# Quarter products in place of full ones in the first layer of seven experts, with the work between the engines set out anew

## The chip, the cores and the metric

The kernel runs on one core of a Trainium2 chip. The metric is the device time of one execution in microseconds (us). The kernel before takes 992.46 us, the median of three runs (991.57 to 992.61).

## The reference, cut to what matters

Local attention gives 4608 tokens of 512 numbers each. A gate then picks two of eight experts for each token, and an expert is two matrix products with a relu between them:

```python
    for e in range(E):
        for k in range(2):
            mask = top2[:, k] == e
            if not mask.any():
                continue
            h = np.maximum(x[mask] @ w1[e], 0.0)
            out[mask] += top2_w[mask, k, None] * (h @ w2[e])
```

All of it is float32: `x` is 4608 x 512, `w1[e]` is 512 x 1024, `w2[e]` is 1024 x 512. About 1152 tokens go to each expert.

## The kernel before, in words

**Stages.** Attention, gate and routing come first and overlap with expert 0. From the middle of expert 0 on TensorE does little but expert products. An expert has a fixed number of places for tokens (`CAPS`, L30): 1216 for the first two, 1184 for three, 1152 for three. More tokens than that go through an extra loop at the end (L844), which runs zero times here; its count `n_over` is worked out in L829 to L843, after the last expert.

**Numbers in two parts.** A float32 operand is split into a high part (a ScalarE copy to `fp32r`) and a low part (a VectorE subtraction, operand minus high part). `three` (L298) multiplies two such operands with three matmuls: high by high, high by low, low by high. Each matmul loads a 128 x 128 piece as weights and streams the other operand past it.

**Blocks.** `blocks_tail` (L51) cuts the list of experts 1 to 7 into three blocks of 384 tokens; what is over 1152 (64 or 32 tokens, the tail) joins the first block. `BL` (L149) is the list of all blocks. Expert 0 has blocks of its own (`blocks_of`, L37), the last one with a tail of 64.

**First layer** (`layer1`, L307): for each of 8 pieces of 128 hidden units, 4 pieces of the 512 inputs, 3 matmuls each, so 96 matmuls in a block, each streaming the block's 384, 416 or 448 tokens. ScalarE applies relu and writes the high part `hh` (L323), VectorE the low part `hl` (L324). A tail's hidden units go to `hf` instead (L321).

**Second layer** (`layer2`, L346): per tile of 128 tokens 24 matmuls of 512 columns. `weigh` (L340) scales the result on VectorE (L343), and `store` (L270) adds it to the output with an indirect DMA that POOL issues (L272). A tail goes through `tail2` (L327) with small matmuls (L334) before the block's tiles.

**What surrounds them.** POOL gathers the tokens ahead of time, four indirect DMAs to a tile (`gather_some`, L248, L260), at most `LEAD` = 7 tiles ahead, in 5 + 3 buffers. `x_tile` (L279) turns a tile on VectorE (L292) and splits it (L295 ScalarE, L296 VectorE). Weights arrive by DMAs that SP issues (`w_load`, L120) into four staging buffers `st`, and are split by `w_split` (L130: L137 ScalarE, L138 VectorE). The order on every engine is the order of the program. The main loop (L751) hands small pieces of this work to hooks that run between groups of matmuls: the tiles of the next block during the first layer or, in the middle block, during the second; the split of `w2` during the first layer of the middle block; the split of the next expert's `w1` in the second layer.

Of the kernel before, what the change touches and what calls it, by code (L numbers as in the profile page):

```python
# [60 lines left out]
def kernel(ctx, tc, qT, kT, vh, wgn, noise, w1, w2, out, caps=CAPS):  # L61
# [4 lines left out]

    xbuf = dram.tile([NROWS, DM], FT, name="xbuf")
# [3 lines left out]
    jp = consts.tile([P, P], FT, name="jp")  # L71
# [3 lines left out]
    before = consts.tile([P, P], BF, name="before")  # L75
    nc.vector.tensor_scalar(before, jp, 0.0, None, op0=OP.is_gt)
    ones = consts.tile([P, P], BF, name="ones")
# [4 lines left out]
    row = consts.tile([P, P], FT, name="row")  # L82
    nc.gpsimd.iota(row, pattern=[[1, P]], base=0, channel_multiplier=0, allow_small_or_imprecise_dtypes=True)
    e_row = row[:, 0:NE]

    row_p = consts.tile([P, P], FT, name="row_p")
    nc.gpsimd.iota(row_p, pattern=[[NE, P]], base=0, channel_multiplier=0, allow_small_or_imprecise_dtypes=True)
    row_je = consts.tile([P, NLIST, NE], FT, name="row_je")
# [52 lines left out]
    pg = ExitStack()  # L141
    gate = pg.enter_context(tc.tile_pool(name="gate", bufs=1, side="right"))
# [5 lines left out]
    assert all(len(b) == nb for b in blocks)  # L148
    BL = [(e, b) for e in range(NE) for b in range(nb)]  # L149
    NBL = len(BL)  # L150
    NJ = NLIST
    BN = max(sum(r for _, r in b) for bs in blocks for b in bs)
    LEAD = 7
# [10 lines left out]
    later_xg = []  # L164
    xg = ctx.enter_context(tc.tile_pool(name="xg", bufs=5))
    bx0 = ctx.enter_context(tc.tile_pool(name="bx0", bufs=1))
# [3 lines left out]
    acc = consts.tile([P, 2, NL], FT, name="acc")  # L170
# [18 lines left out]
    WIDE = {"tr": (0, 1), "l1": (0, 2, 3, 4), "l2": (1, 5, 6, 7)}  # L189

    def bank(what, among=None):
        among = among or (BANKS if rot["l2"] < 6 else WIDE)[what]
# [86 lines left out]
    def x_tile(i, k, at=None):  # L279
# [5 lines left out]
        if i < NPE:  # L285
            src = (bank("tr") if at is None else PS[:, at, :]).rearrange("p (d n) -> p d n", d=ND)[:, :, 0:r]
            for d in range(ND):
                nc.tensor.transpose(src[:, d, :], x[0:r, d * P:(d + 1) * P], ident[0:r, 0:r])  # L288
            oh, ol = xh[:, :, s], xl[:, :, s]
        else:  # L290
            y = xy.tile([P, DM], FT, name="y")
            nc.vector.transpose(y[:, 0:4 * r], x[:, 0:4 * r])  # L292
            src = y[:, 0:4 * r].rearrange("p (t b c) -> p b t c", b=ND, c=32)
            oh, ol = (a[:, :, s].rearrange("p b (t c) -> p b t c", c=32) for a in (xh, xl))
# [3 lines left out]
    def three(p, w, w_s, x, x_s, first, last, flip=False):  # L298

        (wh, wl), (xh, xl) = w, x  # L300
        for n, (a, b) in enumerate(((wh, xh), (wh, xl), (wl, xh)) if not flip else ((wh, xh), (wl, xh), (wh, xl))):
# [3 lines left out]
            nc.tensor.matmul(p, a, b, start=first and n == 0, stop=last and n == 2)  # L305

    def layer1(i, hook, hook_d=lambda f, d: None):  # L307
# [3 lines left out]
        for f in range(NF):  # L311
# [645 lines left out]
```

## Time and profile before

| | |
|---|---|
| median of 3 runs | 992.46 us |
| the profiled execution: its own time | 993.31 us |
| its span, first to last instruction | 991.5 us |
| TensorE matmul busy (PE) | 953.3 us, 96% |
| weight loads (PEld) | 854.4 us, 86% |
| VectorE (DVE) | 458.3 us, 46% |
| ScalarE (ACT) | 307.8 us, 31% |
| GpSimd (POOL) | 485.2 us, 49% |
| granted TensorE clock, mean | 0.991 |

PE is matmul and PEld weight load, both on TensorE. The busy time of an engine is the time in which at least one of its instructions is on record as running. Matmuls are pipelined: the record of one lasts until its end, while the next has already begun, so the pace of TensorE is read from starts and not from durations. `L305` is line 305 of the kernel; since every expert matmul is recorded in `three`, they all have this one line and are told apart by their tiles and widths. A span of 1.00 in the column PEclk is the full 2.4 GHz.

### The profile page before, as it was taken

Reading aid. Unit: us, or ns where it says so; the run is one execution under the profiler, and the core shown is the slowest. Engines: PE = TensorE matmul, PEld = TensorE weight load, DVE = VectorE, ACT = ScalarE, POOL = GpSimd, SP = SyncE. Lnnn points to the kernel's source line nnn. Section 1 sums busy time; section 2 is a strip of 40 time slices with the busy share of each in tenths; the row PEclk is TensorE's granted clock in tenths of the full one; section 3 lists DMA queues with packets and bytes.
Section 4 is the critical chain, followed back from the end, with each engine's and each line's share of the span. In section 5 each row is a group of like instructions: output and inputs, shape, how many; then the busy total and the mean of one; then the engine's idle time right before and its main releaser. Section 6 shows DMA issues by size and latency. Waiting matters only on the chain.

```text
span 991.5 us, 18556 instructions
## 1 busy us (share of the span) xinstructions
PE 953.3 (96%) x7353; PEld 854.4 (86%) x7353; DVE 458.3 (46%) x1001; ACT 307.8 (31%) x689; POOL 485.2 (49%) x619
## 2 busy tenths in 40 slices
PE   6788989999999999999999999999999999999995
PEld 5666779998798998998899899989998999899984
DVE  6678876643444442534253435343444344434311
ACT  4667865312232321322132213122312231223100
POOL 1033635426677876177517772676167616601111
PEclk9999999999999999999999999999999999999998
DMA  9998968332513462245214522552245224511213
GB/s 330 376 308 299 317 224 326 63 114 57 144 47 85 108 152 49 47 120 149 51 35 128 149 49 37 134 141 58 70 94 141 58 71 94 136 20 22 32 23 43
DMA packets 60362, 121.54 MB, mean 123 GB/s; under 512 B 9280, under 2 KB 10176, under 8 KB 60272
## 3 DMA queue, kind: packets, MB, share of 16 engines
q1 hardware_dynamic: 40112, 81.64, 23.3%
q0 software_dynamic: 20160, 38.69, 21.0%
q8 instruction: 58, 0.95, 0.4%
q14 instruction: 32, 0.26, 0.1%
HBM read 81.56 MB, written 38.73 MB: 121 GB/s over the span
## 4 chain that ended last, share of the span: by engine, by line
PE 84%; DVE 1%; issue 0%
PE PS L305 82%; PE PS L334 1%; PE PS L590 1%; PE PS L288 0%; DVE gmi L518 0%; PE PS L222 0%; PE PS L464 0%; PE PS L476 0%; DVE o L343 0%; DVE xs L449 0%; PE PS L224 0%; DVE gm L514 0%; PE PS L457 0%; DVE nf L836 0%; PE PS L537 0%
## 5 line engine op out<-in xcount | busy, mean ns | idle before, releaser
L260 POOL DMA_INDIRECT xg<-xbuf,piece x257 | 265.9, 1035 | 71.4 <-issue 65.0
L305 PE MATMUL PS<-xh,w1h 128*128 128x384 f32 (+2 forms) x768 | 263.1, 343 | 0.0
L305 PE MATMUL PS<-xh,w1l 128*128 128x384 f32 (+2 forms) x768 | 260.8, 340 | 0.0
L305 PE MATMUL PS<-xl,w1h 128*128 128x384 f32 (+2 forms) x768 | 260.7, 339 | 0.0
L272 POOL DMA_INDIRECT out<-o,lid x73 | 116.1, 1591 | 244.2 <-DVE o L343 232.7
L305 PE MATMUL PS<-w2h,hh 128*128 128x512 f32 x584 | 228.6, 391 | 0.0
L305 PE MATMUL PS<-w2h,hl 128*128 128x512 f32 x584 | 227.7, 390 | 0.0
L305 PE MATMUL PS<-w2l,hh 128*128 128x512 f32 x584 | 227.5, 390 | 0.0
L323 ACT ACTIVATE hh<-PS 128x384 fp32r<-128x384 f32 (+1 forms) x192 | 93.9, 490 | 362.3 <-PE PS L305 361.5
L324 DVE SCALAR_TENSOR_TENSOR hl<-PS,hh 128x384 fp32r<-128x384 f32 (+1 forms) x192 | 106.9, 558 | 180.8 <-ACT hh L323 180.8
L343 DVE TENSOR_SCALAR o<-PS,lwt 128x512 f32<-128x512 f32 x73 | 54.7, 749 | 233.5 <-PE PS L305 233.5
L305 PEld LDWEIGHTS PS<-xh,w1h 128*128 128x128 f32 x768 | 144.7, 188 | 2.7 <-issue 0.8
L305 PEld LDWEIGHTS PS<-xl,w1h 128*128 128x128 f32 x768 | 144.7, 188 | 1.8
L305 PEld LDWEIGHTS PS<-xh,w1l 128*128 128x128 f32 x768 | 144.5, 188 | 1.0
L305 PEld LDWEIGHTS PS<-w2h,hl 128*128 128x128 f32 x584 | 109.2, 187 | 23.6
L305 PEld LDWEIGHTS PS<-w2h,hh 128*128 128x128 f32 x584 | 109.2, 187 | 23.1 <-issue 0.8
L305 PEld LDWEIGHTS PS<-w2l,hh 128*128 128x128 f32 x584 | 109.2, 187 | 22.4
L295 ACT ACTIVATE xh<-y 128x512 fp32r<-128x512 f32 x67 | 41.2, 615 | 105.1 <-DVE y L292 105.1
L296 DVE TENSOR_TENSOR xl<-y,xh 128x512 fp32r<-128x512 f32 x67 | 44.9, 671 | 48.0 <-ACT xh L295 48.0
L598 POOL TENSOR_SCALAR gohp<-row_p,gpf 128x128 f32<-128x128 f32 x36 | 24.8, 721 | 85.0 <-DVE gpf L582 76.7
L292 DVE STREAM_TRANSPOSE y<-xg 128x512 f32<-128x512 f32 x67 | 45.6, 680 | 3.5 <-DMA xg<-xbuf,piece 3.5
L138 DVE TENSOR_TENSOR w2l<-st,w2h 128x512 fp32r<-128x512 f32 x64 | 44.3, 693 | 0.0
(139 smaller groups left out, 780.6 us busy)
## 6 DMA issues: line engine op xcount, KB each, us to landing
st<-in_w SPq DMA_DIRECT2D x56, 512.0 KB, 3.4
out<-zero SPq DMA_DIRECT2D x37, 256.0 KB, 3.3
vb<-in_vh SPq DMA_DIRECT2D x36, 260.0 KB, 4.7
qp<-in_qT SPq DMA_DIRECT2D x36, 256.0 KB, 5.6
kb<-in_kT SPq DMA_DIRECT2D x36, 256.0 KB, 5.7
xbuf<-xs SPq DMA_DIRECT2D x36, 256.0 KB, 4.3
xg<-xbuf,piece POOLq DMA_INDIRECT x257, 2.8
st<-in_w SPq DMA_DIRECT2D x16, 256.0 KB, 4.2
```

The lines of the kernel that those rows point to most:

```text
L138: (eng or nc.vector).tensor_sub(lo[:, s], st[:, s], hi[:, s].bitcast(FT))
L260: nc.gpsimd.indirect_dma_start(out=XG[e, j][:, t * P:(t + 1) * P], out_offset=None, in_=xpieces, in_offset=bass.IndirectOffsetOnAxis(ap=pi ...
L272: s = nc.gpsimd.indirect_dma_start(out=to, out_offset=bass.IndirectOffsetOnAxis(ap=rows, axis=0), in_=o, in_offset=None, compute_op=OP.add)
L292: nc.vector.transpose(y[:, 0:4 * r], x[:, 0:4 * r])
L295: nc.scalar.activation(oh, src, AF.Copy)
L296: nc.vector.tensor_sub(ol, src, oh.bitcast(FT))
L305: nc.tensor.matmul(p, a, b, start=first and n == 0, stop=last and n == 2)
L323: nc.scalar.activation(hh[:, 0:m], p, AF.Relu)
L324: nc.vector.scalar_tensor_tensor(hl[:, 0:m], p, 0.0, hh[:, 0:m].bitcast(FT), op0=OP.max, op1=OP.subtract)
L334: nc.tensor.matmul(p[32 * q:32 * q + 32, 0:P], HF[0][:, f, 32 * t:32 * t + 32], w[:, q * P:(q + 1) * P], start=(f == 0), stop=(f == NF - 1))
L343: nc.vector.tensor_scalar(o[0:r], p[0:r], weights_of(i, j)[0:r], None, op0=OP.mult)
L598: nc.gpsimd.tensor_scalar(ohp[:, 0], row_p, pf[:, 0, 0, r:r + 1], None, op0=OP.is_equal)
```

## The change

Experts 1 to 7 compute their first layer by seven products of quarter matrices in place of eight. The 512 x 1024 matrix `w1` is cut in four (inputs by hidden units), a block of tokens in four (inputs by tokens), and sums of quarters are multiplied: Strassen's scheme in the form with fifteen additions. Four of the additions are on quarters of `w1` and four on quarters of the tokens, the others are on results.

- An expert has two blocks in place of three: 512 tokens and the tail, and 640 tokens. Each half of the tokens is 256 (288 or 272 with the tail's half), or 320 wide. `layer1s` runs, for each of seven products `m`, four pieces `f` of 128 hidden units, two pieces `d` of the inputs, three matmuls.
- Products accumulate in two chains of PSUM banks, `a` in banks 0 to 3 and `b` in banks 4 to 7 (`CHAIN`). Between two products of chain `a` ScalarE copies a bank to a buffer `u`; VectorE adds chain `b` to `u`, and relu and low part are made from the sum. A tail's part of a sum goes through POOL.
- `weights_work` and `rows_work` list the additions and splits as small tasks, and the loop over blocks hands them out at given steps of both layers (`SPLITS`, `TASKS`, and the spacings 1.6 and 0.7). The whole of the next block's rows but three splits is made in a second layer; the three (`rows_later`) at steps 5, 9 and 20 of the first layer that uses them.
- `weigh` scales on ScalarE from the last block of expert 0 on. `tail2` comes after the first tile. `LEAD` is 5 in place of 7 and all gathered tiles use the 5 buffers.
- The count of overflowing rows is computed on VectorE after the routing and not after the last expert; the load of the count and the branch stay where they were.
- Buffers of the gate and of the constants move to a pool that is closed after the routing. Expert 0's own first layer is as before.

```diff
...
-    full = [(j, P) for j in range(cap // P)]
-    out = [full[n:n + 3] for n in range(0, len(full), 3)]
-    if cap % P:
-        out[0] = out[0] + [(cap // P, cap % P)]
-    return out
+    assert cap // P == 9
+    tail = [(9, cap % P)] if cap % P else []
+    return [[(j, P) for j in range(4)] + tail, [(j, P) for j in range(4, 9)]]
...
-            W[e, which, c] = (wpool.tile([P, 1024], FR, name=f"w{which}h{c}"),
-                              wpool.tile([P, 1024], FR, name=f"w{which}l{c}"))
+            h, l = (f"a{c}", f"a{4 + c}") if which == 1 else (f"w2h{c}", f"w2l{c}")
+            W[e, which, c] = wpool.tile([P, 1024], FR, name=h), wpool.tile([P, 1024], FR, name=l)
...
-    BN = max(sum(r for _, r in b) for bs in blocks for b in bs)
-    LEAD = 7
+    BN = max(sum(r for _, r in b) for b in blocks[0])
+    LEAD = 5
...
-        n = rot["xg"] = rot["xg"] + (i >= NPE)
-        XG[e, blocks[e][b][k][0]] = (later_xg[0] if n % 8 in (1, 2, 3) and i >= NPE else xg).tile([P, DM], FT, name="xg")
+        XG[e, blocks[e][b][k][0]] = xg.tile([P, DM], FT, name="xg")
...
-            r = blocks[e][b][-1][1] % P if e else 0
-            m = n - r
-            if r:
-                nc.scalar.activation(HF[0][:, f, 0:r], p[:, m:n], AF.Relu)
-                p = p[:, 0:m]
-            nc.scalar.activation(hh[:, 0:m], p, AF.Relu)
-            nc.vector.scalar_tensor_tensor(hl[:, 0:m], p, 0.0, hh[:, 0:m].bitcast(FT), op0=OP.max, op1=OP.subtract)
+            nc.scalar.activation(hh[:, 0:n], p, AF.Relu)
+            nc.vector.scalar_tensor_tensor(hl[:, 0:n], p, 0.0, hh[:, 0:n].bitcast(FT), op0=OP.max, op1=OP.subtract)
...
-        nc.vector.tensor_scalar(o[0:r], p[0:r], weights_of(i, j)[0:r], None, op0=OP.mult)
+        if i >= NPE - 1:
+            nc.scalar.activation(o[0:r], p[0:r], AF.Copy, scale=weights_of(i, j)[0:r])
+        else:
+            nc.vector.tensor_scalar(o[0:r], p[0:r], weights_of(i, j)[0:r], None, op0=OP.mult)
         store(e, out, rows_of(i, j)[0:r], o[0:r])
 
-    def layer2(i, hook):
+    def layer2(i, hook, hh, what=None):
         e, b = BL[i]
-        tiles = blocks[e][b]
-        if e and tiles[-1][1] < P:
-            tail2(e, *tiles[-1])
-            tiles = tiles[:-1]
-        for k, (j, r) in enumerate(tiles):
-            p = bank("l2")
+        tail = [t for t in blocks[e][b] if e and t[1] < P]
+        for k, (j, r) in enumerate(t for t in blocks[e][b] if t not in tail):
+            p = bank("l2", (k,) if e else None)
             for f in range(NF):
                 three(p[0:r], W[e, 2, f // 2], (slice(None), slice((f % 2) * DM, (f % 2) * DM + DM)),
-                      HT[i][f], (slice(None), slice(k * P, k * P + r)), f == 0, f == NF - 1, flip=True)
+                      hh[f], (slice(None), slice(k * P, k * P + r)), f == 0, f == NF - 1, flip=True)
                 hook(k, f)
             weigh(i, j, r, p)
+            if k == 0 and tail:
+                tail2(e, *tail[0])
             if i > 1:
                 gather_some(2)
...
+    M = {"11": 0, "12": 1, "s2": 2, "s1": 3, "s3": 4, "22": 5, "s4": 6}
+    CHAIN = [("a", True), ("b", True), ("a", False), ("b", True), ("a", False), ("a", False), ("b", False)]
...
+    def split(hi, lo, src):
+        nc.scalar.activation(hi, src, AF.Copy)
+        nc.vector.tensor_sub(lo, src, hi.bitcast(FT))
...
+        V = nc.vector
+        work = [t for both in zip(cut(M["11"], a11), sums(V.tensor_add, a21, a21, a22)) for t in both]
+        work += sums(V.tensor_sub, a11, a21, a11)
+        work += cut(M["12"], a12)
+        work += cut(M["s2"], a11)
+        work += cut(M["s1"], a21)
+        work += sums(V.tensor_sub, a21, a22, a11)
+        work += cut(M["s3"], a21) + load((0, 1))
+        work += sums(V.tensor_sub, a12, a12, a11)
+        work += cut(M["22"], a22)
+        work += cut(M["s4"], a12) + load((2, 3))
+        return work
...
+        def turn(k):
+            def run():
+                j, r = blocks[e][b][k]
+                gathered(i, k)
+                nc.vector.transpose(base[:, 4 * k:4 * k + r // 32].rearrange("p t b c -> p (t b c)"), XG[e, j][:, 0:4 * r])
+                ahead[0] -= 1
...
+        first = [turn(k) for k in range(len(blocks[e][b]))]
+        first += [cut(M["11"], q[0, 0]), cut(M["12"], q[1, 0]),
+                  diff(q[0, 0], q[0, 1], q[0, 0]),
+                  diff(q[0, 1], q[1, 1], q[0, 1]),
+                  cut(M["s1"], q[0, 0]),
+                  diff(q[0, 0], q[1, 1], q[0, 0]),
+                  cut(M["s2"], q[0, 0]),
+                  diff(q[1, 0], q[1, 0], q[0, 0])]
+        return first, [cut(M["s3"], q[0, 1]), cut(M["22"], q[1, 0]), cut(M["s4"], q[1, 1])]
...
+            def run():
+                nc.scalar.activation(hh[:, s], src[:, 0:n0], AF.Relu)
+                to = HF[0][:, f, h * r2:h * r2 + r2]
+                if r2 and pool:
+                    nc.gpsimd.tensor_scalar(to, src[:, n0:n], 0.0, None, op0=OP.max)
+                elif r2:
+                    nc.scalar.activation(to, src[:, n0:n], AF.Relu)
...
+        for m, (chain, first) in enumerate(CHAIN):
+            for f in range(4):
+                a, c = PS[:, f, 0:n], PS[:, 4 + f, 0:n]
+                for d in range(2):
+                    three(a if chain == "a" else c, [w.rearrange("p (d f) -> p d f", d=2) for w in WS[e, m]],
+                          (slice(None), d, slice(f * P, (f + 1) * P)),
+                          TS[i, m], (slice(None), d, slice(0, n)), first and d == 0, d == 1, skip=True)
+                if m in (0, 2, 4):
+                    u[m, f] = pools["u"].tile([P, 320], FT, name="u")
+                    nc.scalar.activation(u[m, f][:, 0:n], a, AF.Copy)
+                if m == 1:
+                    out(0, f, added(u[0, f], c))
+                elif m == 4:
+                    out(1, 4 + f, added(u[4, f], c))
+                elif m == 5:
+                    out(0, 4 + f, a, False)
+                elif m == 6:
+                    out(1, f, added(u[2, f], c))
+                drain(1)
+                work(4 * m + f)
+        drain(0)
...
+            nf = consts.tile([1, NE], FT, name="nf")
+            nc.vector.tensor_sub(nf, run8[0:1], e_row[0:1])
+            nc.vector.tensor_scalar(nf, nf, 1.0 / NE, float(P - 1), op0=OP.mult, op1=OP.add)
+            nc.vector.tensor_sub(nf, nf, cape)
...
+    for name, bufs in (("wb", 1), ("t", 4), ("base", 1), ("ob", 3), ("u", 9)):
+        pools[name] = ps.enter_context(tc.tile_pool(name=f"s{name}", bufs=bufs, side="right"))
...
+    SPLITS = (2, 3, 6, 10, 12, 13, 14, 15)
+    TASKS = (12, 13, 14, 15, 17, 19, 21, 23, 25)
...
+    for i in range(NPE - 1, NBL):
+        e, b = BL[i]
+        last = b == len(blocks[e]) - 1
+        steps = 8 * sum(r == P or e == 0 for _, r in blocks[e][b])
+        if i >= NPE:
+            follow = rows_later
+
+            def work(q):
+                if q in (5, 9, 20):
+                    follow.pop(0)()
+                if b == 0 and q in SPLITS:
+                    w_split(e, 2, *halves[SPLITS.index(q)])
+                if last and ww and q in TASKS:
+                    ww.pop(0)()
+                if q % 2:
+                    gather_some(1, HS[0][0] if q == 5 else None)
+
+            if last and e + 1 < NE:
+                ww = weights_work(e + 1)
+            layer1s(i, work)
+        if i + 1 < NBL:
+            rows_first, rows_later = rows_work(i + 1)
+        else:
+            rows_first = []
+        tasks = [(1 + 1.6 * n, t) for n, t in enumerate(rows_first)]
+        if last and e + 1 < NE:
+            ww = ww if e else weights_work(e + 1)
+            tasks += [((0.7 * steps if e else steps - 2) * n / len(ww), t) for n, t in enumerate(ww)]
+            ww = []
+            tasks.sort(key=lambda a: a[0])
+        elif e and e + 1 < NE:
+            for c in (0, 2, 1, 3):
+                w_load(e + 1, 1, c)
+        spread_over(i, tasks)
+        layer2(i, lambda k, f: run_due(i, 8 * k + f), HS if e else HT[i])
+        run_due(i, 10 ** 6)
...
-    nf = ovp.tile([1, NE], FT, name="nf")
-    nc.vector.tensor_sub(nf, run8[0:1], e_row[0:1])
...
```

## Rows read from the trace of the kernel before

**Rows 1.** The page: busy time of each engine, whole span.

```profile
PE 953.3 (96%) x7353; PEld 854.4 (86%) x7353; DVE 458.3 (46%) x1001; ACT 307.8 (31%) x689; POOL 485.2 (49%) x619
```

**Rows 2.** Windows: window, its length, busy PE, PEld, DVE, ACT, POOL (instructions), PEclk, DMA, GB/s.

```profile
376.00:479.00 103.00, 103.00 (x573) 94.00 (x573) 42.40 (x70) 26.16 (x58) 60.53 (x77) 1.00 0.37 90
...
781.00:880.00 99.00, 99.00 (x506) 90.46 (x505) 41.24 (x68) 25.14 (x49) 43.26 (x54) 1.00 0.35 84
```

**Rows 3.** Timeline of PE (start, duration in us), matmuls with which a layer begins.

```profile
247.44 0.40 PE L305 MATMUL PS<-w2h,hh 128*128 128x512 f32 x1
...
269.30 0.36 PE L305 MATMUL PS<-xh,w1h 128*128 128x448 f32 x1
...
288.75 0.34 PE L305 MATMUL PS<-xh,w1h 128*128 128x384 f32 x1
...
325.62 0.33 PE L305 MATMUL PS<-xh,w1h 128*128 128x384 f32 x1
...
342.29 0.39 PE L305 MATMUL PS<-w2h,hh 128*128 128x512 f32 x1
...
358.65 0.35 PE L305 MATMUL PS<-xh,w1h 128*128 128x416 f32 x1
...
376.57 0.39 PE L305 MATMUL PS<-w2h,hh 128*128 128x512 f32 x1
```

**Rows 4.** Timeline of weight loads: two of layer 1, then eight ahead of 16-column matmuls.

```profile
500.33 0.19 PEld L305 LDWEIGHTS PS<-xh,w1h 128*128 128x128 f32 x1
500.50 0.19 PEld L305 LDWEIGHTS PS<-xl,w1h 128*128 128x128 f32 x1
...
139.13 0.97 PEld L476 LDWEIGHTS PS<-sel,ls 128*128 128x128 f32 x8
```

**Rows 5.** Lines by form, 376.57 to 478.96 (one expert's period): busy us, mean ns.

```profile
L324 DVE SCALAR_TENSOR_TENSOR hl<-PS,hh 128x384 fp32r<-128x384 f32 x24 | 13.3, 555 | 22.5 <-ACT hh L323 22.5
L323 ACT ACTIVATE hh<-PS 128x384 fp32r<-128x384 f32 x24 | 11.7, 488 | 42.0 <-PE PS L305 42.0
...
L343 DVE TENSOR_SCALAR o<-PS,lwt 128x512 f32<-128x512 f32 x9 | 6.7, 750 | 30.1 <-PE PS L305 30.1
L292 DVE STREAM_TRANSPOSE y<-xg 128x512 f32<-128x512 f32 x9 | 6.3, 703 | 0.0
L296 DVE TENSOR_TENSOR xl<-y,xh 128x512 fp32r<-128x512 f32 x9 | 6.2, 692 | 6.6 <-ACT xh L295 6.6
L295 ACT ACTIVATE xh<-y 128x512 fp32r<-128x512 f32 x9 | 5.7, 632 | 14.5 <-DVE y L292 14.5
...
L321 ACT ACTIVATE hf<-PS 128x32 f32<-128x32 f32 x8 | 1.5, 190 | 18.8 <-PE PS L305 18.8
...
L296 DVE TENSOR_TENSOR xl<-y,xh 128x128 fp32r<-128x128 f32 x1 | 0.3, 293 | 0.4 <-ACT xh L295 0.4
```

**Rows 6.** Timeline of DVE: like instructions merged, total of the run and their count.

```profile
207.85 1.48 DVE L324 SCALAR_TENSOR_TENSOR hl<-PS,hh 128x384 fp32r<-128x384 f32 x3
...
254.79 1.29 DVE L138 TENSOR_TENSOR w1l<-st,w1h 128x512 fp32r<-128x512 f32 x2
```

**Rows 7.** Timeline of all engines after the last matmul, 979.14.

```profile
979.57 0.75 DVE L343 TENSOR_SCALAR o<-PS,lwt 128x512 f32<-128x512 f32 x1 [4.69 <-PE PS L305]
980.23 0.14 DVE L830 TENSOR_TENSOR nf<-run,row 1x8 f32<-1x8 f32 x1
...
980.60 1.55 POOL L272 DMA_INDIRECT out<-o,lid  x1 [3.85 <-DVE nf L831]
...
982.03 0.14 DVE L841 CAST toti<-tot 1x1 int32<-1x1 f32 x1
```

**Rows 8.** DMA issues: count, size, median us from issue to landing.

```profile
st<-in_w SPq DMA_DIRECT2D x56, 512.0 KB, 3.4
...
out<-o,lid POOLq DMA_INDIRECT x73, 4.9
```

**Rows 9.** Timeline of DVE after the routing: [idle before, and what ended it].

```profile
213.47 0.75 DVE L343 TENSOR_SCALAR o<-PS,lwt 128x512 f32<-128x512 f32 x1 [3.81 <-PE PS L305]
```

More of the change, by code (lines that the diff above doesn't have):

```diff
@@ L74 @@
     nc.vector.tensor_scalar(ident, jp, 0.0, None, op0=OP.is_equal)
-    before = consts.tile([P, P], BF, name="before")
+    before = gate.tile([P, P], BF, name="before")
     nc.vector.tensor_scalar(before, jp, 0.0, None, op0=OP.is_gt)
-    ones = consts.tile([P, P], BF, name="ones")
+    ones = gate.tile([P, P], BF, name="ones")
     nc.vector.memset(ones, 1.0)
@@ L284, in x_tile, with three @@
         s = slice(k * P, k * P + r)
[L285 to L294, printed above, removed]
+        src = (bank("tr") if at is None else PS[:, at, :]).rearrange("p (d n) -> p d n", d=ND)[:, :, 0:r]
+        for d in range(ND):
+            nc.tensor.transpose(src[:, d, :], x[0:r, d * P:(d + 1) * P], ident[0:r, 0:r])
+        oh, ol = xh[:, :, s], xl[:, :, s]
         nc.scalar.activation(oh, src, AF.Copy)
         nc.vector.tensor_sub(ol, src, oh.bitcast(FT))
-    def three(p, w, w_s, x, x_s, first, last, flip=False):
+    def three(p, w, w_s, x, x_s, first, last, flip=False, skip=False):
         (wh, wl), (xh, xl) = w, x
@@ L304, in three @@
                 a, b = b, a
-            nc.tensor.matmul(p, a, b, start=first and n == 0, stop=last and n == 2)
+            nc.tensor.matmul(p, a, b, start=first and n == 0, stop=last and n == 2,
+                             skip_group_check=skip)
     def layer1(i, hook, hook_d=lambda f, d: None):
@@ new lines, in halves_of, with rows_work, quarter, parts @@
+    def halves_of(i):
+        tail = sum(r for _, r in blocks[BL[i][0]][BL[i][1]] if r < P)
+        return (256, tail // 2) if BL[i][1] == 0 else (320, 0)
+    def rows_work(i):
+        e, b = BL[i]
+        n0, r2 = halves_of(i)
+        g = n0 // 32
+        base = pools["base"].tile([P, 20, ND, 32], FT, name="base")
+        def quarter(dh, rh):
+            ds_ = slice(2 * dh, 2 * dh + 2)
+            out = [base[:, rh * g:rh * g + g, ds_, :].rearrange("p g b c -> p b g c")]
+            if r2 == 32:
+                out.append(base[:, 2 * g + rh, ds_, :])
+            elif r2:
+                out.append(base[:, 2 * g, ds_, rh * r2:rh * r2 + r2])
+            return out
+        def parts(t):
+            out = [t[:, :, 0:n0].rearrange("p b (g c) -> p b g c", c=32)]
+            return out + ([t[:, :, n0:n0 + r2]] if r2 else [])
+        def ops(m):
+            if (i, m) not in TS:
+                TS[i, m] = tuple(pools["t"].tile([P, 2, 320], FR, name=n) for n in ("th", "tl"))
+            return TS[i, m]
+        def turn(k):
[4 more added lines that the diff above has]
+                ahead[0] -= 1
+            return run
+        def diff(out, x, y):
+            def run():
+                for o, p, q in zip(*(v() for v in (out, x, y))):
+                    nc.vector.tensor_sub(o, p, q)
+            return run
+        def cut(m, src):
+            def run():
+                hi, lo = ops(m)
+                for h, l, s in zip(parts(hi), parts(lo), src()):
+                    split(h, l, s)
+            return run
+        q = {(d, r): (lambda d=d, r=r: quarter(d, r)) for d in range(2) for r in range(2)}
+        first = [turn(k) for k in range(len(blocks[e][b]))]
[7 more added lines that the diff above has]
+        return first, [cut(M["s3"], q[0, 1]), cut(M["22"], q[1, 0]), cut(M["s4"], q[1, 1])]
@@ L388 @@
             load_v(t - 1)
[L389 removed]
+    wg = gate.tile([P, ND, 32], FT, name="wg")
     nc.sync.dma_start(wg, wgn)
[L391 removed]
+    nz = gate.tile([P, NT, NE], FT, name="nz")
     nc.sync.dma_start(nz, noise)
[L394 removed]
+    zero = gate.tile([P, DM], FT, name="zero")
     nc.gpsimd.memset(zero, 0.0)
@@ new lines, with spread_over, run_due @@
+    pb.close()
+    ps = ExitStack()
+    for name, bufs in (("wb", 1), ("t", 4), ("base", 1), ("ob", 3), ("u", 9)):
+        pools[name] = ps.enter_context(tc.tile_pool(name=f"s{name}", bufs=bufs, side="right"))
+    OB[0] = pools["ob"]
+    todo = {}
+    ww = []
+    SPLITS = (2, 3, 6, 10, 12, 13, 14, 15)
+    TASKS = (12, 13, 14, 15, 17, 19, 21, 23, 25)
+    def spread_over(i, tasks):
+        todo[i] = [(int(at), t) for at, t in tasks]
+    def run_due(i, at):
+        while todo.get(i) and todo[i][0][0] <= at:
+            todo[i].pop(0)[1]()
```

149 lines of the change are left out of this document (81 added, 68 removed).

## The prediction

> **What bounds the kernel now.** I read the page's busy times first [rows 1]: TensorE's matmuls are busy 96% of the span, VectorE 46%, ScalarE 31%. That alone says little, since the share is a mean over attention, routing and experts. So next the windows, one expert each [rows 2]: matmuls run 103.00 of 103.00 us and 99.00 of 99.00, at granted clock 1.00, which is the 2.4 GHz level, while VectorE works 42.40 and 41.24 us and POOL 60.53 and 43.26. In experts 1 to 7 TensorE alone sets the time and nothing makes it wait. Then the pace, from the starts at which layers begin [rows 3]: 96 first-layer matmuls take 16.67 us at 384 columns (325.62 to 342.29), 17.92 at 416, 19.45 at 448; 72 second-layer ones of 512 take 16.36. That is 173.6, 186.7, 202.6 and 227.2 ns each: a line of 0.419 ns a column and 12.8 ns for the matmul itself. So two things cost time: columns and the count of matmuls. The change lowers the first and raises the second.
>
> **Matmuls, removed and added.** Before, an expert's first layer is three blocks: 19.45 + 2 x 16.67 = 52.79 us with a tail of 64, 17.92 + 33.34 = 51.26 with 32, 3 x 16.67 = 50.01 with none. One, three and three experts: 356.6 us. After, a block is 7 products x 4 x 2 x 3 = 168 matmuls, of 288, 272 or 256 columns in the first block and 320 in the second. The line gives 133.4, 126.7, 120.0 and 146.8 ns, so an expert takes 168 x (133.4 + 146.8) ns = 47.07 us, 45.95 or 44.82; together 319.4. The term is **-37.2 us**. Of it columns give -41.4, and 336 more matmuls (2352 for 2016) take 4.3 back. No row has so narrow an `fp32r` matmul, so I bound it: if the fixed part vanished below 384 columns, the term would be -41.4 or a little more; the other end, a floor under the pace, is a rival below. I take the line, since four widths lie on it within 2 ns.
>
> The page "TensorE: Matmul & The Clock Gate" of the Trainium skill (section "Back-to-back issue gap") gives N/2.4 + 2.5 ns for a warm engine. That would be 162.5 ns at 384 columns, against 173.6 here, and the trace disagrees by a fixed 11 ns; by the page the term would be -40.3 us.
>
> The second layer has the same matmuls: 72 tiles less expert 0's, 24 each. `tail2` only moves behind the first tile: 0.
>
> **What VectorE and ScalarE take on.** From [rows 5] a VectorE instruction takes 160 ns + 1.04 a column (293 at 128, 692 at 512), a ScalarE one about 163 + 0.85 (190 at 32, 488 at 384). Back to back VectorE is denser: two of 512 end after 1.29 us, three of 384 after 1.48 [rows 6], so one follows another after 0.60 and 0.46 us. I count by both, as upper and lower bound. Take the experts with a tail of 32:
> - First layer of the first block, 21.3 us of TensorE: 12 additions of 272, 16 low parts of 256, 3 row splits (512 + 32), 8 of `w2`: 5.3 + 6.8 + 2.7 + 5.5 = 20.3 us of VectorE by durations, 16.1 by the dense pace.
> - First layer of the second block, 24.7 us: 12 additions and 16 low parts of 320, 3 splits of 640, 9 weight tasks: 5.9 + 7.8 + 2.5 + 6.2 = 22.4, or 18.5.
> - Both second layers, 49.1 us: 9 tiles and a tail turned (6.6), 8 row splits and 8 row sums (13.6), 13 weight tasks (9.0): some 29.6.
>
> That is 72 us of the 97 that the expert will last (45.95 + 216 x 0.2272 + 1.9 for its tail), where it was 42.4 of 102.4. ScalarE comes to some 54 us by the same counting. No stage asks more of VectorE than it lasts, so the sums go beside the matmuls: 0, as long as the first-layer stages keep that cover of 1.0 to 2.3 us; beyond it each us of VectorE is one of TensorE.
>
> **Waits added.** TensorE now waits for the other engines inside a block. A bank of chain `a` is written again four steps later at the closest (product 4 to 5), with three steps of matmuls, 2.2 to 2.6 us, to cover a ScalarE copy of 0.4: 0. The closest operand is the last split of rows, issued at step 20 and used from step 24: four steps, 3.5 us in a second block, for 0.71 us on ScalarE and then 0.83 on VectorE. A backlog of 1.9 us there makes TensorE wait. In steps 16 to 19 VectorE gets 4 additions, 4 low parts and 2 tasks, 5.3 us by durations and 4.3 by the dense pace, for 3.5 us of matmuls: a backlog of 1.8 or 0.8 us, and ScalarE's queue stands behind additions as well. So the wait lies between nothing and some 1 us in a second block, less in a first. I take 0.3 us in each of seven second blocks, nearer to the dense pace: **+2 us**. When that operand is late, the second layer is not late in turn: its first tile needs product 5's parts only after four more groups.
>
> **Other moves.** `weigh` goes from VectorE (0.75) to ScalarE (0.60 estimated at 512 columns); only the last one is on the path: 0 to -0.2, I take 0. Behind a `weigh` that waits for its tile, ScalarE's splits for the next block queue, one tile of 5.5 us at most, and they are due in the next first layer: 0. The row count: nine small VectorE instructions from 980.23 to 982.17, while POOL's last store is issued until 982.15 and lands about 4.9 us after its issue [rows 7, 8]. The store ends the kernel, so removing them gives 0 (bound -1.9); behind the routing they fall in VectorE's idle 3.81 us [rows 9]: 0 (bound +1.9). Weight loads: `w1` is now issued ahead of the first block's second layer, over 21 us before its first task; the last `w2` loads fall at step 28 of 40, 12 steps of 0.68 us ahead of the next block, against 3.4 us to land [rows 8]: 0. On SP nothing but weights queues behind them. POOL's gathers stay the same in number, with 5 buffers for 8; 14 in a first layer and 8 to 10 in a second make the 17 to 20 that a block needs, so they are in before VectorE turns them: 0. Its dozen small tail pieces per first block are needed a tile (5.5 us) later. The changeover from expert 0: 22 weight tasks and 13 row tasks, 25.7 or 21.5 us of VectorE, in a second layer of 21.86 [rows 3]; the rest is due 10 us later: 0, at worst 2.
>
> **Sum.** The profiled execution took 993.3 us (its span 991.5 and 1.8 around it): 993.3 - 37.2 + 2 = 958.1. The median of the runs lies 0.85 lower, so I predict **957 us**.
>
> **Rivals.**
> - *Late operands.* VectorE is the tight one; with instructions 15% longer than the rows under the denser traffic, the second block asks 25.8 us of 24.7 and the first 23.3 of 21.3: 3.1 us an expert, 22 in all, some 977. For it: 95% by durations in the first block. Against: the dense pace leaves a quarter free. 970 to 990, chance 0.13. If waits came to 2.65 us in each of 14 blocks, nothing would be left: no change, 0.02, which is also what a scheme that did not cut the columns would give.
> - *A floor under the weight loads (slower).* Every matmul needs its own load of 128 columns, and the change adds 336. Place: the first layer. If loads can't follow each other faster than some floor, narrow matmuls gain nothing; from 356.6 / 2352 = 151.6 ns on the change loses. At 173.6, the closest `fp32r` loads on record [rows 4], it costs 2352 x 0.1736 - 356.6 = +52 us, 1044. Against: eight loads ahead of 16-column matmuls take 0.97 us with the last one's 0.19, so 0.111 us apart [rows 4], under all four new paces. Chance 0.04.
> - *Load time as occupancy (slower).* An expert with a tail of 32 now has 504 such loads at 0.188 us, 94.8 us of its 102.4. With 552 it would be 103.8 and the tail's 1.9: 3.3 us more in place of 5.3 less, about +23 in all, 1015. Against: loads start 0.17 apart and last 0.19 [rows 4], so records overlap and their sum is no occupancy. Chance 0.02. This is the measure of the page "Perfetto Trace Analysis" of the Trainium skill (section "Identifying the Most-Contended Engine"), which judges TensorE by the busy share of weight loads; the trace speaks against that reading here.
>
> **How the numbers follow.** The forecast, 951 to 970, has 0.77: its low end is -41.4 without waits, its high end 1 us of waits in each of 14 blocks in place of 2 in all. Faster than 951 gets 0.02. I reach a little into the late operands, to 973, to hold 8 in 10. Some 0.2%, 2 us, is what runs of this kernel can tell from no change. Faster: 0.77 + 0.13 + 0.02 = 0.92; same 0.02; slower 0.06.
>
> **What would show it.** Right: first-layer matmuls 120 to 147 ns apart, a first layer of 20.2 to 22.4 and 24.7 us, second-layer starts at 227 ns, VectorE near 72 us an expert, no new wait of TensorE over 1 us. Wrong: paces that don't fall with the width (the floor), or first layers longer than 168 paces, with TensorE waiting for VectorE or ScalarE (late operands); and a tail after the last matmul that is shorter by 2 us would say the count was on the path after all.

## The result, and the profile after

The changed kernel took 957.67 us (median of 4 runs, 955.61 to 962.68), the kernel before 992.02 beside it: a ratio of 0.9663 [0.9621, 0.9705]. The forecast was 957.0. The record doesn't name the chip of this first measurement. Measured again later, on chip 6, the same kernel came out slower than the kernel before. Both results are told here, the first measurement first.

The profiled execution took 955.61 us, its span 953.7. Busy times of the engines over the whole span, from the page of the changed kernel, to be held against [rows 1]:

```profile
PE 914.1 (96%) x7689; PEld 815.6 (86%) x7689; DVE 596.0 (62%) x1388; ACT 466.8 (49%) x1065; POOL 498.7 (52%) x578
```

TensorE lost 39.2 us of busy time with 336 more matmuls; VectorE and ScalarE gained 138 and 159 us and the span did not follow them. Next the windows of five first layers of the changed kernel (columns as in [rows 2]): first and second block of an expert with a tail of 32, a second block of an expert without tail, and both blocks of the last expert.

```profile
368.33:389.42 21.09, 21.09 (x170) 21.09 (x168) 16.04 (x38) 16.10 (x46) 17.08 (x23) 1.00 0.26 58
413.30:438.35 25.05, 24.91 (x169) 24.64 (x168) 15.91 (x33) 15.11 (x34) 12.84 (x15) 1.00 0.31 88
702.05:727.03 24.98, 24.91 (x169) 24.61 (x168) 15.99 (x32) 15.09 (x34) 16.27 (x17) 1.00 0.22 53
848.06:867.89 19.83, 19.83 (x170) 19.79 (x169) 15.15 (x35) 15.25 (x38) 10.69 (x13) 1.00 0.23 50
889.74:914.38 24.64, 24.64 (x170) 24.64 (x168) 12.63 (x27) 13.45 (x31) 1.59 (x2) 1.00 0.08 11
```

A first layer is 168 matmuls: 21.09 us are 125.5 ns each at 272 columns, 19.83 are 118.0 at 256, 24.64 are 146.7 at 320. The forecast had 126.7, 120.0 and 146.8. The second blocks with another expert behind them take 0.3 to 0.9 us more than the last one, which has none. All fourteen first layers sum to 322.1 us, of which 4.5 are over these paces. From the start of expert 0's last second layer to the end of the last matmul it is 697.3 us, where it was 731.9: **-34.6**, against the forecast's -35.2. The stage before that came out 3.1 us shorter, in attention, whose instructions the change leaves as they are; why isn't shown. The median of the four runs lies 2.06 above the profiled one.

The waits of the changed kernel, 244 to 942 us (in total, times, longest):

```profile
DVE u L490 <- ACT u L502: 8.5, 7, 4.7
...
DVE st L379 <- DMA st<-in_w: 5.6, 4, 2.0
...
ACT w2h L138 <- DMA st<-in_w: 3.2, 1, 3.2
PEld PS L296 <- DVE tl L358: 3.0, 7, 0.8
```

TensorE's only wait of size is on `tl`, the low part of rows, from the last split of a second block: the operand that the prediction named. The other three are waits of VectorE and ScalarE. Two places in the timeline of VectorE show what they were (columns: start, duration, last the idle time before it and what ended it):

```profile
273.01 1.51 DVE L139 TENSOR_TENSOR w2l<-st,w2h 128x512 fp32r<-128x512 f32 x2 [4.05 <-ACT w2h L138]
...
428.59 0.69 DVE L379 TENSOR_TENSOR st<-st 128x512 f32<-128x512 f32 x1 [1.55 <-DMA st<-in_w]
429.20 0.48 DVE L490 TENSOR_TENSOR u<-u,PS 128x320 f32<-128x320 f32 x1
429.60 0.48 DVE L470 SCALAR_TENSOR_TENSOR ls<-u,hs 128x320 fp32r<-128x320 f32 x1
430.00 0.48 DVE L490 TENSOR_TENSOR u<-u,PS 128x320 f32<-128x320 f32 x1
```

At 273.01 VectorE had stood for 4 us in expert 1's first block: the split of `w2` waited for a load issued at 266.11 that landed at 272.32. That block, which began at 266.16, took 24.36 us where its pace asks 22.4. The load was issued so late because it needs a staging buffer that VectorE's `w1` tasks still read. SyncE, which issues the loads, had stood before it from 196.8 to 266.0 us, the longest of these waits of its queue (total, times, longest):

```profile
SPq L127 <- DVE st L379: 406.7, 13, 69.2
```

VectorE ended that `w1` sum at 265.95 and the last of expert 1's `w1` tasks at 268.96, and the last two `w2` loads were issued only at 268.39 and 269.02. At 428.59 a `w1` sum waited for its load. And the starts 0.40 apart, with 0.48 on record for each, are the dense pace at 320 columns.

The end of the changed kernel (timeline of all engines from the last matmul on), against [rows 7]:

```profile
941.40 0.39 PE L296 MATMUL PS<-w2h,ls 128*128 128x512 f32 x1
941.87 0.69 ACT L331 ACTIVATE o<-PS,lwt 128x512 f32<-128x512 f32 x1 [4.75 <-PEq L1024]
942.84 1.55 POOL L269 DMA_INDIRECT out<-o,lid  x1 [3.85 <-ACT o L331]
```

The last store is issued 1.44 us after the last matmul began; it was 1.46. With the count gone from the end, the end is as long as before.

### The profile page after: what moved, and what is told of

The parts are those of the page before. It is cut to its first block, busy times and chain, and to the rows that moved or that the text cites. A ratio compares the mean times of both kernels' runs of the same rounds, so it can differ in the third digit from the quotient of the medians.

```text
span 953.7 us, 19926 instructions
## 1 busy us (share of the span) xinstructions
PE 914.1 (96%) x7689; PEld 815.6 (86%) x7689; DVE 596.0 (62%) x1388; ACT 466.8 (49%) x1065; POOL 498.7 (52%) x578
## 4 chain that ended last, share of the span: by engine, by line
PE 57%; DMA 11%; issue 8%; DVE 5%; POOL 2%; ACT 1%; SPq 0%; POOLq 0%; DVEq 0%; ACTq 0%
PE PS L296 54%; DMA st<-in_w 10%; POOL out L269 1%; DVE u L490 1%; DVE ls L470 1%; POOL xg L257 1%; PE PS L743 1%; PE PS L321 1%; DVE tl L358 1%; DVE st L379 1%; ACT w2h L138 0%; ACT u L502 0%; SPq L125 0%; PE PS L284 0%; DMA xg<-xbuf,piece 0%
## 5 line engine op out<-in xcount | busy, mean ns | idle before, releaser
L296 PE MATMUL PS<-w2h,hs 128*128 128x512 f32 x504 | 196.6, 390 | 0.0
L296 PE MATMUL PS<-w2l,hs 128*128 128x512 f32 x504 | 196.3, 389 | 0.0
L296 PE MATMUL PS<-w2h,ls 128*128 128x512 f32 x504 | 196.2, 389 | 0.0
L296 PE MATMUL PS<-th,a 128*128 128x320 f32 (+3 forms) x896 | 183.7, 297 | 0.2 <-DVE u L490 0.2
L296 PEld LDWEIGHTS PS<-th,a 128*128 128x128 f32 x896 | 145.4, 188 | 1.0 <-DVE u L490 0.4
L296 PE MATMUL PS<-tl,a 128*128 128x320 f32 (+3 forms) x448 | 133.1, 297 | 0.0
L296 PEld LDWEIGHTS PS<-w2h,hs 128*128 128x128 f32 x504 | 94.6, 188 | 19.9 <-issue 0.8
L296 PE MATMUL PS<-tl,b 128*128 128x320 f32 (+3 forms) x336 | 100.8, 300 | 1.3 <-DVE tl L358 0.9
L296 PE MATMUL PS<-th,b 128*128 128x320 f32 (+3 forms) x336 | 100.2, 298 | 0.6 <-ACT th L357 0.6
L296 PE MATMUL PS<-th,c 128*128 128x320 f32 (+3 forms) x336 | 100.0, 298 | 0.0
```

## The experiments

They ran in three groups, on chips 6, 5 and 10, each group beside the kernel before; a ratio is always to those runs. The changed kernel without an edit ran again on chip 6 alone, so a comparison with it from chip 5 or 10 is also one between chips. Two runs are left out of the figures, one of `extra_14` (3180 us) and one of the kernel before (4019): they took three and four times as long as the others, and nothing shows why.

### The same kernel again, and where it went

`after_again` is the changed kernel without any edit.

> The changed kernel once more, beside the next three on one chip. Theory (the gain is the columns of the first layer): ratio to the kernel before 0.966 within 0.004, first layers of 19.8, 21.1 and some 24.9 us, and the stage from expert 0's last second layer to the last matmul again 697 us in the profile. Rival (part of the gain is chance in the attention stage, where the profile of the changed kernel was 3 us ahead): the time comes out 2 to 5 us higher while the expert stage stays at 697.

Measured: 1013.61 us (six runs, 1009.61 to 1017.67) where the kernel before took 1000.67: 1.0124 [1.0098, 1.0150]. The kernel before is 9 us slower than in the first measurement, the changed one 56, and the gain has become a loss. Neither forecast came: most of the loss is in the expert stage, 750.3 us long in place of 697.3. Windows of the second blocks of experts 4, 6 and 7 in `after_again`:

```profile
634.07:667.65 33.58, 29.34 (x169) 27.52 (x168) 16.34 (x34) 15.52 (x35) 16.30 (x19) 0.85 0.26 71
845.08:878.05 32.97, 27.45 (x169) 25.98 (x168) 15.87 (x33) 14.88 (x34) 16.12 (x17) 0.90 0.19 40
949.51:974.15 24.64, 24.64 (x169) 24.63 (x168) 12.62 (x27) 13.44 (x31) 1.59 (x2) 1.00 0.09 12
```

The last expert's block, in which POOL has two instructions, takes the 24.64 us of the first measurement to the hundredth. The other two take 33 with the same busy time on VectorE and ScalarE (16.00 and 15.10 us in the same block of expert 6 before, 795.88 to 820.86). The first layers sum to 374.5 us, 52.4 more. What `after_again` waits for, 250 to 1003 us:

```profile
DVE u L490 <- ACT u L502: 45.0, 14, 8.4
...
ACT u L502 <- remote: 41.1, 10, 10.0
...
PE PS L296 <- ACT u L502: 14.2, 7, 4.3
PE PS L296 <- issue: 13.4, 23, 1.4
```

ScalarE's copies `u` wait for something that the profile calls remote, a signal whose sender it can't name, and TensorE and VectorE wait for the copies. In the last row, issue is time in which TensorE stood and waited for nothing that the profile shows; the first measurement has no such row for matmuls. The worst place, expert 6's second block, in the timeline of `after_again`:

```profile
864.26 0.95 POOL L257 DMA_INDIRECT xg<-xbuf,piece  x1 [0.30 <-issue]
865.51 0.94 POOL L257 DMA_INDIRECT xg<-xbuf,piece  x1 [0.30 <-issue]
...
868.43 0.44 ACT L502 ACTIVATE u<-PS 128x320 f32<-128x320 f32 x1 [8.59 <-remote]
...
868.90 0.49 DVE L490 TENSOR_TENSOR u<-u,PS 128x320 f32<-128x320 f32 x1 [7.05 <-ACT u L502]
868.92 0.63 PE L296 MATMUL PS<-th,b 128*128 128x320 f32 x1 [4.13 <-ACT u L502]
```

The group of matmuls that the copy at 868.43 takes over had ended at 860.2. TensorE's semaphore updates for that group and the next ones, up to 864.8, are on record at 868.40 to 868.63, all together, right after the last gather had landed (867.72). So ScalarE was told 8.2 us late, TensorE came to the end of what it could do, and the clock fell to its 1.2 GHz level during the wait (PEclk 0.90 in the window): behind it matmuls start 0.27 us apart until 871.75, in place of 0.147.

TensorE also stood where it had nobody to wait for, in the same stretch:

```profile
862.67 0.41 PE L296 MATMUL PS<-th,c 128*128 128x320 f32 x1 [0.41 <-issue]
...
864.10 0.41 PE L296 MATMUL PS<-th,b 128*128 128x320 f32 x1 [0.40 <-issue]
```

Both lie inside a group of six and have no wait of their own, and each starts 0.7 us after the matmul before it. In `after_again` sixteen such stops cost some 12.7 us over the pace. And only TensorE's signals are late: between 244 us and the last matmul, 104 of its 398 updates on record come more than 0.15 us after the end of a matmul that sends one (4 of 442 in the first measurement), against none of VectorE's 710 and none of ScalarE's 586. So by these records what is slow sits with TensorE and not with the two engines that it hands over to.

The same step of the same block in the changed kernel's first timeline, under the same gathers:

```profile
808.37 1.40 POOL L257 DMA_INDIRECT xg<-xbuf,piece  x1 [0.30 <-issue]
810.07 0.94 POOL L257 DMA_INDIRECT xg<-xbuf,piece  x1 [0.30 <-issue]
811.07 0.44 ACT L502 ACTIVATE u<-PS 128x320 f32<-128x320 f32 x1 [2.92 <-PE PS L296]
811.32 0.95 POOL L257 DMA_INDIRECT xg<-xbuf,piece  x1 [0.30 <-issue]
812.01 0.44 ACT L502 ACTIVATE u<-PS 128x320 f32<-128x320 f32 x1
```

Gathers follow each other as closely, and the copies come as the groups end. Over all 168 copies the lag from the end of a group (or of ScalarE's work before it) is at most 0.12 us in the first measurement. In `after_again` it goes to 8.3 and sums to 77 us; the ten copies with no gather packets within 1 us lag by 0.10 at most. In the second blocks of experts 1 to 6 the last burst of updates comes 0.06 to 0.88 us after the last packet of a run of gathers. So the lateness goes with the gathers, but the gathers alone don't make it.

### Does more slack help, and less cost more?

`last_split_17` issues the last row split three steps sooner, so it has seven steps and not four; `w2_splits_late` delays expert 1's `w2` splits; `three_mends` has both and `w1` loads in four parts (below). Same chip as `after_again`.

```diff
-                if q in (5, 9, 20):
+                if q in (5, 9, 17):
...
+    SPLITS_1 = (8, 9, 11, 12, 13, 15, 21, 23)
...
-                if b == 0 and q in SPLITS:
+                at = SPLITS_1 if e == 1 else SPLITS
+                if b == 0 and q in at:
```

> The last split of rows is issued at step 17 in place of 20. Theory (VectorE's backlog makes this one operand late): the waits of 0.3 to 0.4 us in each second block go, second blocks of experts 1 to 6 fall from 24.9 to 25.5 to about 24.7 us, 2 us in all. Rival (VectorE is held up by the late load of w1, so the place of the split doesn't matter): they stay.

> Expert 1 alone splits w2 at steps 8 to 23 in place of 2 to 15. Theory (its w2 lands only at steps 7 to 15, and ScalarE and VectorE stand behind the first split): the first block of expert 1 falls from 24.4 to about 22.4 us, 2 us in all. Rival (VectorE's own backlog from the changeover): it stays above 24.

> Both of these and w1 loaded in four pieces of 32 rows each. Theory: the three waits are apart from each other, so the expert stage falls by 4 to 4.5 us to some 693, and w1's last piece lands within 20 us of its first issue in place of 30. Rival (the waits move to the next operand): less than 2 us.

Measured: `last_split_17` 1003.62, 1.0022 [0.9999, 1.0045], 10 us better than `after_again`, and its interval lies clear of the other. Second blocks of experts 1 to 3 fell from 28.8 to 27.0 us, of 4 to 6 from 33.0–33.6 to 32.3–32.9. In `after_again` TensorE's loads waited 6.0 us for `tl` and 3.9 for `th`; with the split sooner the view has neither. So this operand was where slack was missing. VectorE's instructions are as long as in the first measurement, where the place cost 2.5 us, so I put the rest down to the late signals. The second blocks didn't come down to 24.7 us: the waits for late copies are still there. `w2_splits_late` 1007.46, 1.0106 [1.0062, 1.0149]: its target, expert 1's first block, stayed at 23.69 us (23.55), so the edit shows no gain there, and the interval overlaps that of `after_again`. `three_mends` 1003.77, 1.0031 [1.0012, 1.0051]: as `last_split_17`. In its trace expert 1's first block takes 22.28 us and the last part of `w1` lands within 17 us, as forecast, but the expert stage takes 733.5 us and not 693. None beats the kernel before on that chip.

`extra_7` and `extra_14` add a VectorE instruction that reads a constant, at every fourth and every second step of a first layer: 98 and 196 of them. It writes to a new small tile, `scr`, in the pool of the hidden units.

```diff
+                if q % 4 == 1:
+                    nc.vector.tensor_reduce(scr, idw, AX.X, OP.add)
```

> Seven more VectorE instructions of 512 columns in each block's first layer, at every fourth step. If the dense pace counts (0.60 us each, VectorE has 5 to 9 us free in a first layer): only the last split gets later by the one ahead of it, 0.6 us a block, 5 to 9 us in all. If durations count (0.69 us, cover of 1.0 to 2.3 us): 2.5 to 3.8 us a block, about 44 us.

> Fourteen of them, at every second step, 8.4 us a block by the dense pace. Theory: the first blocks ask 24.4 us of 21.1, so they last about 3 us longer, and in second blocks the last split is 1.2 us later: 25 to 35 us in all. If durations count, about 110 us. If VectorE doesn't set TensorE's time at all: none.

VectorE's busy time, from the page of `extra_7`, stands against 597.0 in `after_again`:

```profile
PE 952.7 (93%) x7689; PEld 832.8 (81%) x7689; DVE 651.0 (63%) x1486; ACT 466.9 (45%) x1065; POOL 499.5 (49%) x578
```

98 instructions added 54.0 us of busy time, 0.55 each, and the time rose to 1031.93 (1.0303 [1.0268, 1.0337]), 18 over `after_again`, on another chip. 196 added 113 us and gave 1067.24 in one run, 54 over it. Not all of this is VectorE's work. The second layer of the same block (expert 2's second), to which the edit adds no instruction, in `after_again` and then in `extra_7`:

```profile
454.64:481.89 27.25, 27.25 (x123) 22.53 (x121) 19.61 (x43) 11.84 (x25) 14.89 (x15) 1.00 0.55 126
```

```profile
461.84:489.84 28.00, 28.00 (x123) 22.54 (x121) 21.40 (x46) 12.44 (x26) 14.34 (x14) 1.00 0.51 121
```

In both `extra` runs the second-layer matmuls of experts 1 to 7 start 233.3 ns apart in place of 227.0, over 9 us in all, while expert 0's, which read other tiles, keep 226.9. The new tile may have moved the hidden units in memory; that wasn't tried. What the added work costs is read from the first layers: they sum to 380.6 and 417.7 us where `after_again` has 374.5, so 6 and 43 us. The first lies in the 5 to 9 us of the dense pace; the second is over its 25 to 35 and far from the 110 by durations. On these chips more work on VectorE is no longer free. What slack it had in the first setting was not tried.

### Which cover is short?

`w1_by_rows` loads a piece of `w1` by four DMAs of 32 rows; `tasks_in_layer2` moves the `w1` tasks out of the second block's first layer; `weigh_on_vector` puts `weigh` back on VectorE; `count_at_end` puts the count back behind the last expert. One chip for all four.

```diff
-            nc.sync.dma_start(st, w1v[ds(place[e], 1), c].rearrange("o j r f -> (o j) r f") ...)
+            for j in range(4):
+                nc.sync.dma_start(st[32 * j:32 * j + 32, :], w1v[ds(place[e], 1), c, j] ...)
...
-    TASKS = (12, 13, 14, 15, 17, 19, 21, 23, 25)
+    TASKS = ()
...
-        if i >= NPE - 1:
+        if i < 0:
```

> w1 is loaded in four pieces of 32 rows each in place of one piece cut by four. Theory (the old form lands slowly, 30 us for the four loads of an expert, whatever else runs): all four land within 20 us, VectorE's wait of 1.2 to 2.5 us for the last of them in experts 1 to 4's second blocks goes; TensorE gains only where that was over 2 us, about 0.5 us at expert 4. Rival (POOL's gathers slow all transfers alike): landing stays near 30 us.

> None of the next expert's weight tasks in the second block's first layer: all 26 in the second layer. Theory (the two tasks at steps 17 and 19 are the backlog ahead of the last split): second blocks fall to 24.7 us, 2 us less; in exchange the loads of w2 come as late as step 28 as before, so nothing is lost. Rival (the second layer is then too short and the next expert starts late): some us an expert more.

> Results are scaled on VectorE again from expert 0's last block on. Theory (in the second layers VectorE has some 20 us free): within 1 us in all, waits in the first layers unchanged. Rival (VectorE then turns the next rows later, and operands of the next block are late): 1 us and more a block, over 7 us.

> The count of overflowing rows is computed after the last expert again. Theory (the last store's landing ends the kernel): 0, and 12.1 us between the last matmul and the end, as in both kernels. Rival (the count was on the path): 1.9 us longer.

Measured: 1013.16 (1.0116 [1.0090, 1.0142]), 1015.53 (1.0127 [1.0076, 1.0178]), 1019.41 (1.0183 [1.0166, 1.0200]) and 1010.53 (1.0113 [1.0062, 1.0165]). In the trace of `w1_by_rows` the last parts of an expert's `w1` land 13 to 17 us after the first issue, as far as its updates are on record, in place of 25 to 33 in the first measurement; but the second blocks stay at 28.8 to 33.6 us. So these loads are not what is late. Without the tasks the second blocks take 28.0 to 28.3 and 32.3 to 33.6 us, nearly as with them, so the tasks are not what fills them either. `weigh` on VectorE is unclear: its five runs lie between 1000.27 and 1021.01, and the ratio given stands for the three highest, so I read no size from it. With the count at the end the tail behind the last matmul is 12.6 us, and 12.5 to 12.7 without: 0, as in the first measurement.

### What the products and the columns are worth

`eighth_product` computes the first product twice with the same values, so a block has 192 matmuls. `narrow` leaves out all but the first 192 columns of each half in a first block, and all but 128 in a second.

```diff
-                for d in range(2):
+                for d in (0, 1, 0, 1) if m == 0 else (0, 1):
...
+                    nn = 192 if b == 0 else 128
-                          TS[i, m], (slice(None), d, slice(0, n)), first and d == 0, d == 1, skip=True)
+                          TS[i, m], (slice(None), d, slice(0, nn)), first and d == 0, d == 1, skip=True)
```

> The first product is computed twice in each block (the second time over the first, so the values are the same): 24 more matmuls a block. Theory (what is saved is one product in eight, at the pace of its width): 24 x (118.0, 125.5 or 133 ns) + 24 x 147 ns an expert, 45 us in all, so some 1002 us, above the kernel before. Rival (the gain is the spacing of the work or the larger blocks): clearly less than 45 us more.

> Matmuls of the quarter products stream only 192 columns in first blocks and 128 in second ones (the other columns are left out). Theory (line of 0.419 ns a column and 12 ns, down to a floor of 0.11 us for a load of weights): both widths start about 0.11 us apart inside a group of six. Rival without a floor: 92 and 66 ns. Rival of a higher floor: as far apart as at 256 columns, 0.118 us.

To set the waits apart I took out of each trace's expert stage what the starts of matmuls lie further apart than the pace, where that is over 40 ns; stretches at the lower clock count as waits by this. What is left is TensorE's own work: 731.5 us in the kernel before, 692.3 in the first measurement, 692.9 in `after_again`, 738.2 in `eighth_product`. One product is worth 45.3 us, as the forecast had it (45); cutting the blocks into narrow products costs 6.7 (738.2 - 731.5), where the line of [rows 3] gives 319.4 x 8/7 - 356.6 = 8.4. The difference is the change's 39. The time rose only to 1024.89 (1.0233 [1.0169, 1.0296]), 11 over `after_again`: the waits fell from 57.4 to 21.5 us. The lateness itself is smaller in this trace: the lag of the copies sums to 28 us in place of 77 and is at most 2.8. Whether that is the longer block, other spacing of the gathers or the chip isn't shown. What leaving out the eighth product saves is there in TensorE's own work on these chips too, and goes into the waits.

`narrow` took 1031.77 in one run. Its granted clock, and TensorE in the last expert's second block, at a place where the clock is full:

```profile
core 0: 1030.0 us, clock 0.917
```

```profile
967.47 0.28 PE L296 MATMUL PS<-tl,a 128*128 128x128 f32 x1
967.58 0.38 PE L296 MATMUL PS<-th,a 128*128 128x128 f32 x2
967.80 0.28 PE L296 MATMUL PS<-tl,a 128*128 128x128 f32 x1
967.91 0.39 PE L296 MATMUL PS<-th,a 128*128 128x128 f32 x2
968.14 0.27 PE L296 MATMUL PS<-tl,a 128*128 128x128 f32 x1
```

Every third matmul starts 0.335 us after the last such one, so 0.112 a matmul; at 192 columns it is 0.112 as well, where the line of [rows 3] would give 0.093 and 0.066. There is a floor, and it lies where eight loads of [rows 4] put it, under all paces of the change.

The page "TensorE: Matmul & The Clock Gate" of the Trainium skill (section "Back-to-back issue gap") gives about 81 ns for a sustained matmul of 128 columns with its weight load. With these `fp32r` operands the run shows 112, and the measurement decides. The N/2.4 + 2.5 ns that the prediction held its line against is, by the same section, a gap without the weight load.

## Why the prediction was right, and where it was not

**Matmuls, -37.2: right.** Paces without waits sum to 317.65 us against 356.6, -39.0. The line of [rows 3] held down to 256 columns within 2 ns: it is 0.1 ns high at 320 columns, 1.2 at 272 and 2.0 at 256.

**Floor under the weight loads: refuted as a cost.** The floor was measured at 0.112 us; the narrowest pace here is 0.118. **Load time as occupancy: refuted**: load records cover 86% of the span, as before, and the time fell.

**Waits, +2: place right, size short.** 4.5 us were lost in the first measurement. Second blocks of experts 1 to 6 lost 0.29 to 0.85 us at the last row split, as put. The step that failed is the changeover from expert 0, put at 0 (at worst 2) because what VectorE doesn't finish there "is due 10 us later". But the `w2` loads stand behind that rest, for its staging buffers: VectorE was through with `w1` 2.8 us into expert 1's first layer, the loads were issued from 266.11 to 269.02, and they landed 6 to 9 us after their issue, while their first split was due at step 2. TensorE lost 2 us there, most of it at the same last row split, for which VectorE and ScalarE then came late. This is read from the trace; the edits meant for it ran only where signals were late.

**Other moves, 0: right.** Second layers keep 227 ns a matmul; count and `weigh` show nothing at the end, though `weigh` takes 0.69 us on ScalarE and not 0.60. But the reason given for the `w1` loads, 3.4 us to land, was a median of first parts: the four of an expert take 10, 18, 25 and 30 us, and VectorE waited up to 2 us for the last (the row at 428.59). They took up to 28 us in the kernel before too. The page "DMA: Bandwidth & Descriptors" of the Trainium skill (section "Why a DMA increments its semaphore by 16 and not by 1") says that a DMA uses at most as many engines as its slowest dimension has entries, which is four in this load. The trace agrees: four late updates a load, 16 for `w2`; and split by rows, it landed in about half the time.

**VectorE and ScalarE: right in kind, some ten us high.** From 368.33 to 465.60, one expert, VectorE was busy 62.8 us and ScalarE 48.5, against 72 and 54. The dense pace was the better of the two bounds.

**Late operands, 0.13: it did not happen at first and did in every later run.** That rival put the time at 970 to 990 by instructions 15% longer. In the later measurement the time is 1013.6 with instructions of the same length; what came late were TensorE's signals to ScalarE, and TensorE itself stopped inside groups. The prediction counted on 2.2 to 3.5 us of matmuls to cover each hand-over, and took the hand-over itself as free. That holds at a lag of 0.12 us and falls at 8. The kernel before hands over inside a block too, but there a first-layer bank comes round again after four groups of 12 matmuls, with three of 2.08 us, 6.2 in all, to cover it, and it waits for no sum of two chains. It lost only 9 to 10 us on the later chips; no trace of it there shows where.

**The sum, in part by luck.** It came within 0.7 us of the measured median because misses offset each other: matmuls gave 1.8 us more than forecast and waits took 2.5 more, while the 3.1 us that attention was shorter stand against a median 2.06 above the profiled run.

**Left open.** Why the signals were late in all later runs and never in the first measurement isn't settled. The traces of the later runs also lack a part of the semaphore updates, and the first ones are complete; whether this has the same cause, and whether the recording of the trace itself holds TensorE up, isn't known. Nor was a kernel run without gathers, or the kernel before profiled on the later chips, so that the lateness goes with gathers is shown, and what makes it is not. Whether chip or occasion makes the difference is open as well, and the mends weren't measured in the first setting.

## What to carry to other kernels

Price a smaller matmul by the pace read from starts at several widths, down to a floor that the densest loads of the trace show; that came out within 2 us in 39. But a scheme that trades matmuls for hand-overs between engines is worth only what its cover is worth: count the steps between each producer and its use, and give the shortest the most, since three steps more were worth 10 us where signals ran late. For a load, read what its issue waits for and when its last part lands, not the page's median.

## What was not expected of the hardware

Semaphore updates of TensorE reached ScalarE up to 8.3 us after the matmuls had ended, (10.0 in `narrow`), in bursts around and just after indirect gathers, on three chips and never in the first measurement; those of VectorE and ScalarE were on time in the same traces, and TensorE also stopped for some 0.7 us at a time between matmuls that wait for nothing. The same kernel took 957.67 us in one setting and 1013.61 in another, and the kernel before 992.02 and 1000.67, so a ratio from one setting can have the wrong sign in the next. In the two `extra` runs one small added tile went along with second-layer matmuls 2.8% further apart (233.3 ns for 227.0), at full clock. And during and behind such waits the granted clock fell to the 1.2 GHz level inside the block (0.85 and 0.90 on the mean), which makes a wait dearer than its own length.
